# Linear attention, two blocks on one core: the second block's z finished at q's second unit, its sums behind G's last addition, its kv products two steps later

## The chip, the core and the metric

One NeuronCore of a Trainium2 chip runs the kernel. The metric is the device time of one execution in microseconds (us), given as the median of three timed executions. One further execution was taken with the hardware profiler; its rows are what this document reads. PE is the matrix engine (TensorE), DVE VectorE, ACT ScalarE, POOL GpSimd, SP SyncE. The last two issue most of the DMAs here; "SPq" rows are DMAs issued from SP's queue.

## The reference

Two independent blocks (A and B) of linear attention stand side by side; each has S = 2048 rows, D = 640 columns and H = 32 heads of 20 columns. Cut to what matters:

```
q, k, v = heads(x @ wqkv)
phi(t)  = where(t > 0, t + 1, exp(t)) + 1e-6
kv  = sum over s of phi(k)^T v          # per head, 20 x 20
z   = sum over s of phi(k)              # per head, 20
o   = (phi(q) @ kv) / (phi(q) . z + 1e-6)
out = o @ wo
result = concat(A, B)
```

## The kernel before

All large products run in a split form: each float32 operand is cut into a high and a low part of a reduced format, and three products (high x high, high x low, low x high) are added up in PSUM. So most PE work comes in threes.

**The first part** handles k of both blocks. For each pair of row tiles it forms phi(k) (tiles `ek`, then the split `pkh`, `pkl`), and gathers G = x^T phi(k) block by block: `gstep` (line 517) makes a product of 12 matmuls into a bank `psg`, and DVE adds the bank to `gacc` (line 537). The column sums of phi(k), from which z comes, are gathered by POOL DMAs that add `ek` to `zacc` in SBUF (line 406).

`zsums(b)` (line 592) turns `zacc` into z. Its steps: two DVE additions of halves (`zsum`, line 596); a DVE transpose (`zturn`, line 601); a DVE reduction (`zp`, line 602); a POOL DMA that writes `zp` to DRAM (`zd`, line 606); four POOL DMAs that read it back in another layout (`zq`, line 608); and `finish` (line 613), four small DVE instructions on lines 614 to 617 that make `z` and `zs`. Work of this first part is not emitted in the order written: `note` records jobs with their engine, cost and the tiles that they read and write, and `Plan.emit` lays them out by estimated due times. Its costs and due times set each engine's order, so an added dependence can move other jobs of the same engine.

**The second part** is written out by hand. `qmm(u, c)` (line 1069) computes one of five column blocks c of q for one of eight units u of 512 rows, in five steps k of three matmuls each (`psq`, lines 921 to 923). Units 0 to 3 belong to block A, 4 to 7 to block B. Behind each step, `run("q", u, c, k)` calls whatever `at(...)` placed there; so "(0,1,3)" below is the place behind unit 0, column block 1, step 3. Engines execute their instructions in program order, so an instruction that waits holds up all that stands behind it on the same engine.

Into unit 0 the kernel places block B's kv products: `kvmm2` (line 974) multiplies G by the weights of v for one of six groups of heads (`pskv`, line 981, shown in the trace as ten passes for five matmuls), in one of two PSUM banks (banks 5 and 6, tag "e"); DVE then takes the block diagonal (`kvt`, line 985), ACT and DVE split it (`kvh` line 915, `kvl` line 912). `mmm2` later multiplies the result by wo (`psm`), using a bank of tag "e" too. `wv`, the weights that `kvmm2` reads, stand in seven slots that the loads of unit 1's x (`xqs`, line 952) take over.

For each column block, ACT computes exp and relu of `psq` (lines 1089, 1090), DVE joins them to `pq` (line 1091), and `qacc` adds `pq` times z to `acc` (ACT line 1099 for c = 0, DVE line 1101 for the others). At the next unit's beginning `split_acc` splits `acc` into `ac` (ACT line 915, DVE line 912), and `denmm` makes the denominator from it on PE (`psd`, lines 1111 and 1112) at place (1,1,1). Units 0 to 3 read block A's z; block B's z is read for the first time in unit 4.

Of the kernel before, what the change touches and what calls it, by code (L numbers as in the profile page):

```python
# [12 lines left out]
OP = mybir.AluOpType  # L13
# [64 lines left out]
class Plan:  # L78
# [9 lines left out]
    def note(self, engine, n, fn, w, r, ahead=None, dma=None, late=None, by=None, due=None, safe=0.0, lat=0.0):  # L88
        base = self.RATE.get(engine)
        j = Job(engine, base[0] + base[1] * n if base else n, fn, ahead, dma)  # L90
        for part, writes in [(p, True) for p in w] + [(p, False) for p in r]:
            sp = part.space
            if sp.where is not None and sp not in j.spaces:
                j.spaces.append(sp)
            for lo, hi, other, wrote in sp.uses:
                if lo < part.hi and part.lo < hi and (writes or wrote) and other is not j:
                    j.deps.add(other)
            if writes:
                sp.uses = [u for u in sp.uses if not (part.lo <= u[0] and u[1] <= part.hi and u[2] is not j)]
            sp.uses.append((part.lo, part.hi, j, writes))  # L100
        for d in j.deps:
            d.nexts.append(j)
        for sp in j.spaces:
            sp.left += 1
        if engine == "PE":
            j.ideal = self.pe_at
            self.pe_at += j.cost
        j.late = self.pe_at + (25.0 if late is None else late)
        if by is not None:
            j.late = self.pe_at + by  # L110
        j.by, j.set, j.safe, j.lat = by, due, safe, (LAT if due is None else 1.9) + lat
        self.jobs.append(j)
        return j
# [105 lines left out]
def tile_linear_attn_pair(ctx: ExitStack, tc: tile.TileContext, ins, out: bass.AP):  # L219
# [3 lines left out]
    NC = D // P  # L223
    NT = S // P
    NG = NT // 4
    HF = D // 2
# [55 lines left out]
    note = plan.note  # L282
    MM, MMS = 0.147, 0.105

    G = {(b, c): Space(f"G{c}", D) for b in range(NB) for c in range(NC)}
# [3 lines left out]
    KZ = {b: Space("kz", 1) for b in range(NB)}  # L289
# [108 lines left out]
    zac = {}  # L398
# [118 lines left out]
    def gstep(i, h, c):  # L517
        b, g = divmod(i, NG)
        k = (3, 4, 5)[gn[0] % 3]
        gn[0] += 1  # L520
        tm, rd = [], []
        for j in range(4):
            n = 4 * i + j
            x = tuple(s[c * P:c * P + P] for s in xns[n])
            tm.append((x, pks[n][h]))
            rd += [*x, *pks[n][h]]
        note("PE", MM * 12, lambda: mms(tm, BK[k].open("psg")[:, :HF], True), [BK[k].all], rd)
        go = G[b, c][h * HF:h * HF + HF]

        def keep():  # L530
            if g == 0 and h == 0:
                gacc[b, c] = base.tile([P, D], F32, name="gacc", tag="gacc", bufs=NC)
            o = gacc[b, c][:, h * HF:(h + 1) * HF]
            if g == 0:
                act(o, BK[k].tile[:, :HF], AF.Copy)
            else:
                tt(o, BK[k].tile[:, :HF], o, op=OP.add)  # L537

        note("DVE" if g else "ACT", HF, keep, [go], [BK[k].all])
# [52 lines left out]
    def zsums(b):  # L592

        z, zt32 = Space("zsum", D, ANY), Space("zturn", D, ANY)
        for h in range(2):
            note("DVE", HF, lambda h=h: tt(z.all.f[:, h * HF:h * HF + HF], zac[b][h].all.f[:, :HF],
                                           zac[b][h].all.f[:, HF:], op=OP.add), [z[h * HF:h * HF + HF]], [zac[b][h].all], safe=6.0)
        part, four = Space("zpart", 20), Space("zfour", 20)
        pt, ft4 = zp[b]
        add = dict(axis=mybir.AxisListType.X, op=OP.add)  # L600
        note("DVE", D, lambda: nc.vector.transpose(zt32.all.f, z.all.f), [zt32.all], [z.all])
        note("DVE", D, lambda: nc.vector.tensor_reduce(
            pt.rearrange("p (g c) -> p c g", g=4), zt32.all.f.rearrange("p (c g t) -> p c g t", g=4, t=32), **add),
            [part.all], [zt32.all])
        zdv = Space("zd", 1)
        note("POOL", 1.0, lambda: nc.gpsimd.dma_start(zd[b], pt), [zdv.all], [part.all], dma=0.1, lat=2.0)
        for g in range(4):
            note("POOL", 1.0, lambda g=g: nc.gpsimd.dma_start(
                ft4[g * 32:g * 32 + 32].rearrange("p (q c) -> p q c", q=4),
                zd[b].rearrange("(q i) (g c) -> g i q c", q=4, g=4)[g]), [four[g:g + 1]], [zdv.all], dma=0.1, safe=6.0)  # L610
        zt, s = zz[b]

        def finish():
            nc.vector.tensor_reduce(zt, ft4.rearrange("p (q c) -> p c q", q=4), **add)
            nc.vector.tensor_scalar(zt, zt, S * EPS, None, op0=OP.add)
            nc.vector.tensor_reduce(s, zt, **add)
            nc.vector.tensor_scalar(s, s, EPS, EPS / 4, op0=OP.mult, op1=OP.add)

        note("DVE", 300, finish, [KZ[b].all], [four.all], safe=6.0)

    fd = {}

# [51 lines left out]
    a, z, x = jh[0][0:P], jl[0][0:P], jr[0][0:P]  # L674
# [117 lines left out]
    for p in range(4, NPB):  # L792
        i, h = divmod(p - 2, 2)
# [9 lines left out]
    for p in range(NPB + 1, NP):  # L803
        if p == NPB + 1:
            fl = kvs
        else:
            i, h = divmod(p - NPB - 2, 2)
            gready(NG + i)
            fl = filled(NG + i, h, *((LAST,) if p in (NPB + 2, NP - 1) else ()))
        for q, n, g, k in place:  # L810
            if q == p - NPB:
                fl.setdefault(n, []).append((mmm, g, k))
        kpair(p, fl)
        if p == NPB + 4:
            zsums(0)
        if p == NPB + 4:
            m_forms()
# [13 lines left out]
    for h in range(2):  # L831
        for c in range(NC):
            gstep(LG, h, c)
    zsums(1)

    wst, whl, wvt, xt, xts = {}, {}, {}, {}, {}

# [60 lines left out]
    def bank(name, tag="one", bufs=3):  # L898
        at, n = ptags[tag]
        pn[tag] = pn.get(tag, -1) + 1  # L900
        return psum.tile([P, 512], F32, name=name, tag=f"bank{at + pn[tag] % n}", bufs=1)
# [25 lines left out]
    def at(slot, f, *a):  # L927
        todo.setdefault(slot, []).append((f, a))
# [337 lines left out]

    for g in range(NGR):
        at(("q", 0, 0, 0), load_o, 1, g)
        at(("q", 0, (0, 0, 1, 1, 2, 2)[g], (0, 3, 0, 3, 0, 3)[g]), kvmm2, 1, g)
        at(("q", 0, 1 + g, 1) if g < 4 else ("q", 1, 0, 2 * g - 7), split_o, 1, g)  # L1270
        at((("q", 0, 2, 2), ("q", 0, 3, 2), ("q", 0, 4, 4), ("q", 0, 4, 4), ("q", 1, 1, 2), ("q", 1, 2, 2))[g], mmm2, 1, g)
        at((("q", 0, 2, 4), ("q", 0, 3, 4), ("q", 1, 0, 1), ("q", 1, 0, 3), ("q", 1, 1, 4), ("q", 1, 2, 4))[g],
           store_m, nc.gpsimd)
# [13 lines left out]
    h = NG - 1  # L1287
# [8 lines left out]
    for c in range(NC):  # L1296
        at(("q", 0, (0, 0, 1, 1, 2)[c], (1, 4, 1, 4, 1)[c]), load_xraw, 1, c)
        at(("q", 0, 4, c - 1) if c else ("q", 0, 3, 3), load_xq, 1, c)
        at(("q", 0, 4, c) if c else ("q", 0, 3, 4), round_xq, 1, c)
        for u in range(1, NU - 1):  # L1300
            at(("q", u, 3, c), load_xraw, u + 1, c)
            at(("q", u, 4, c), load_xq, u + 1, c)
            at(("o", u - 1, 2 * c + 4), round_xq, u + 1, c)

    den[0] = bank("psd", "small", 1)

# [93 lines left out]
```

## Time and profile before

| what | value |
|---|---|
| median of 3 timed executions | 579.86 us (579.19 to 580.07) |
| the profiled execution | 581.08 us |
| its span, first to last instruction | 579.3 us |
| busy PE / DVE / ACT / POOL | 567.1 / 434.3 / 341.4 / 63.1 us |
| DMA | 117.64 MB, mean 203 GB/s |
| mean granted PE clock | 0.994 |

The span is what the rows of the trace cover; what lies around it (581.08 - 579.3 = 1.78 us) is start and end of the program. A row of the timeline gives start, duration, engine, line, operation, the tiles, and in brackets the idle time of the engine before it with what ended it. Matmuls overlap in the pipeline, so the time that one takes out of PE is read from start to start rather than from its duration.

### The profile page before, as it was taken

How to read it: one execution, taken by the hardware profiler on the slowest of the kernel's cores; microseconds unless marked ns; L12 is line 12 of the kernel's file. 1: busy time of each engine (PE TensorE's matmuls, PEld its weight loads, DVE VectorE, ACT ScalarE, POOL GpSimd, SP SyncE). 2: the span in 40 equal slices, each digit the busy share in tenths (PEclk: the TensorE clock that was granted, in tenths of full speed). 3: DMA queues.
4: the chain of work that ended last, by engine and by line, in shares of the span. 5: the costliest groups of instructions: out<-in, count | busy, mean ns of one | idle time of the engine just before them, and what ended most of it. 6: DMA issues, size and time to landing. Idle time of an engine off the chain costs nothing.

```text
span 579.3 us, 9490 instructions
## 1 busy us (share of the span) xinstructions
PE 567.1 (98%) x3524; PEld 537.5 (93%) x3524; DVE 434.3 (75%) x706; ACT 341.4 (59%) x619; POOL 63.1 (11%) x103
## 2 busy tenths in 40 slices
PE   8999999999999999999959999999999999999997
PEld 6999999999999999999948889898998989898997
DVE  6788687698788758987615599967789776757792
ACT  6878566574787857676215765755657364545541
POOL 0210011110011111111010101211011200001010
PEclk9999999999999999999989999999999999999999
DMA  8994755858759488798956895664273996122022
GB/s 295 348 287 117 198 143 144 231 142 250 251 132 272 141 234 251 217 283 261 335 145 212 298 324 175 221 234 150 75 267 110 333 392 241 69 74 92 0 92 91
DMA packets 68321, 117.64 MB, mean 203 GB/s; under 512 B 6804, under 2 KB 30132, under 8 KB 68276
## 3 DMA queue, kind: packets, MB, share of 16 engines
q1 hardware_dynamic: 59060, 89.94, 47.5%
q0 software_dynamic: 8928, 26.92, 16.7%
q8 instruction: 27, 0.44, 0.3%
q10 hardware_dynamic: 288, 0.20, 0.1%
q14 instruction: 18, 0.15, 0.1%
HBM read 71.13 MB, written 35.41 MB: 184 GB/s over the span
## 4 chain that ended last, share of the span: by engine, by line
PE 95%; DMA 3%; DVE 1%; POOL 0%; SPq 0%; issue 0%; ACT 0%; DVEq 0%
PE psg L316 24%; PE pa L1200 12%; PE ka L316 10%; PE psq L921 8%; PE psq L922 8%; PE psq L923 8%; PE pe L1200 6%; PE ke L316 5%; PE psk L716 4%; PE psb L1200 4%; PE kb L316 3%; DMA zd<-zp 1%; DMA wk<-in_A_wk 1%; PE pskv L556 1%; PE psm L583 1%; PE pskv L981 1%
## 5 line engine op out<-in xcount | busy, mean ns | idle before, releaser
L316 PE MATMUL psg<-pkl,xnh 128*128 128x320 f32 x320 | 98.9, 309 | 0.0
L316 PE MATMUL psg<-pkh,xnh 128*128 128x320 f32 x320 | 98.8, 309 | 0.0
L316 PE MATMUL psg<-pkh,xnl 128*128 128x320 f32 x320 | 98.5, 308 | 0.0
L921 PE MATMUL psq<-xqh,wh 128*128 128x512 f32 x200 | 79.0, 395 | 0.0
L922 PE MATMUL psq<-xql,wh 128*128 128x512 f32 x200 | 78.4, 392 | 0.0
L923 PE MATMUL psq<-xqh,wl 128*128 128x512 f32 x200 | 78.3, 391 | 0.0
L316 PEld LDWEIGHTS psg<-pkl,xnh 128*128 128x128 f32 x320 | 60.1, 188 | 0.0
L316 PEld LDWEIGHTS psg<-pkh,xnl 128*128 128x128 f32 x320 | 60.1, 188 | 0.0
L316 PEld LDWEIGHTS psg<-pkh,xnh 128*128 128x128 f32 x320 | 60.0, 188 | 0.0
L489 ACT ACTIVATE kt<-ka 128x320 f32<-128x320 f32 x52 | 22.7, 437 | 54.4 <-PE ka L316 54.3
L1215 ACT ACTIVATE o<-pa 128x320 f32<-128x320 f32 x64 | 27.9, 438 | 45.3 <-PE pa L1200 45.0
L406 POOL DMA_DIRECT2D zacc<-ek x32 | 26.6, 842 | 236.6 <-DVE ek L499 173.6
L1091 DVE SCALAR_TENSOR_TENSOR pq<-eq,rq 128x512 f32<-128x512 f32 x40 | 27.6, 691 | 30.5 <-ACT rq L1090 30.4
L537 DVE TENSOR_TENSOR gacc<-psg,gacc 128x320 f32<-128x320 f32 x60 | 29.2, 489 | 23.9 <-PE psg L316 23.1
L1089 ACT ACTIVATE eq<-psq 128x512 f32<-128x512 f32 x40 | 23.9, 597 | 36.4 <-PE psq L923 34.1
L923 PEld LDWEIGHTS psq<-xqh,wl 128*128 128x128 f32 x200 | 37.8, 189 | 8.1
L921 PEld LDWEIGHTS psq<-xqh,wh 128*128 128x128 f32 x200 | 37.9, 190 | 7.3
L922 PEld LDWEIGHTS psq<-xql,wh 128*128 128x128 f32 x200 | 37.9, 189 | 7.2
L401 ACT ACTIVATE pkh<-ek,epst 128x640 fp32r<-128x640 f32 x32 | 26.5, 828 | 8.2 <-DVE ek L499 7.1
L1200 PE MATMUL pa<-fh,dah 128*128 128x320 f32 x96 | 29.7, 309 | 0.0
L1200 PE MATMUL pa<-fh,dal 128*128 128x320 f32 x96 | 29.7, 309 | 0.0
L1200 PE MATMUL pa<-fl,dah 128*128 128x320 f32 x96 | 29.7, 309 | 0.0
(215 smaller groups left out, 1560.1 us busy)
## 6 DMA issues: line engine op xcount, KB each, us to landing
zacc<-ek POOLq DMA_DIRECT2D x32, 320.0 KB, 4.9
xql<-xd SPq DMA_DIRECT2D x40, 256.0 KB, 4.8
xd<-xl SPq DMA_DIRECT2D x29, 320.0 KB, 4.2
out<-o POOLq DMA_DIRECT2D x28, 320.0 KB, 3.6
xns<-in_A_x SPq DMA_DIRECT2D x16, 320.0 KB, 5.4
xts<-in_B_xt_tiles SPq DMA_DIRECT2D x16, 320.0 KB, 3.8
xns<-in_B_x SPq DMA_DIRECT2D x16, 320.0 KB, 5.4
xqs<-in_A_xt SPq DMA_DIRECT2D x20, 256.0 KB, 5.9
```

The costliest lines, as they stand in the source:

```text
L316: nc.tensor.matmul(o, a.r, w.r, start=start and k == i == 0, stop=k == n - 1 and i == 2, skip_group_check=True)
L401: note("ACT", n + 110, lambda: act(hi.r, p.f, AF.Identity, bias=epst), [hi], [p, K0.all], by=8.0)
L406: note("POOL", 1.0, lambda: nc.gpsimd.dma_start(z.f, p.f, **kw), [z], [p], dma=1.0 if first else 1.86)
L537: tt(o, BK[k].tile[:, :HF], o, op=OP.add)
L716: nc.tensor.matmul(o[h][:, :HF], x[a].r, w[c][h * HF:h * HF + HF].r, start=c == 0 and i == 0, stop=c == NC - 1 and i == 2, skip_group_chec ...
L921: nc.tensor.matmul(o, whi, xhi, start=first, stop=False)
L922: nc.tensor.matmul(o, whi, xlo, start=False, stop=False)
L923: nc.tensor.matmul(o, wlo, xhi, start=False, stop=last)
L1089: nc.scalar.activation(e, ps, AF.Exp)
L1091: nc.vector.scalar_tensor_tensor(pq[u][:, c, :], e, 1.0, r, op0=OP.min, op1=OP.add)
L1200: nc.tensor.matmul(ps, x, y, start=start and n == i == 0, stop=n == len(terms) - 1 and i == 2, skip_group_check=True)
L1215: copy = lambda x, y: nc.scalar.activation(x, y, AF.Copy)
```

## The change

For block B alone (b = 1), the two `zsum` additions get a dependence on the last column block of G, so they stand behind the last addition to `gacc`. `finish` is no longer a job of the plan for block B: `zsums` returns it, and it is called at place (1,0,0), behind the first step of q's second unit. The six kv products move from the places (0,0,0), (0,0,3), (0,1,0), (0,1,3), (0,2,0), (0,2,3) to (0,0,2), (0,1,0), (0,1,3), (0,2,0), (0,2,3), (0,3,0).

```
-                                           zac[b][h].all.f[:, HF:], op=OP.add), [z[h * HF:h * HF + HF]], [zac[b][h].all], safe=6.0)
+                                           zac[b][h].all.f[:, HF:], op=OP.add), [z[h * HF:h * HF + HF]],
+                 [zac[b][h].all] + ([G[1, NC - 1].all] if b else []), safe=6.0)
...
-        note("DVE", 300, finish, [KZ[b].all], [four.all], safe=6.0)
+        if b == 0:
+            note("DVE", 300, finish, [KZ[b].all], [four.all], safe=6.0)
+        return finish
...
-    zsums(1)
+    z_end = zsums(1)
...
-        at(("q", 0, (0, 0, 1, 1, 2, 2)[g], (0, 3, 0, 3, 0, 3)[g]), kvmm2, 1, g)
+        at(("q", 0, (0, 1, 1, 2, 2, 3)[g], (2, 0, 3, 0, 3, 0)[g]), kvmm2, 1, g)
...
+    at(("q", 1, 0, 0), z_end)
```

Lines of the changed kernel have higher numbers behind the edit: `zturn` is line 602 there, `z` lines 615 to 618, `kvl` and `ac` line 915, `kvt` line 988, `pq` line 1094, `acc` line 1104, `psq` lines 924 to 926, `pskv` line 984.

DVE, from the last weight split of block A's q (`wl`) to the first products of unit 0, before:

```order
L858 TENSOR_TENSOR wl<-wq,wh 128x640
L537 TENSOR_TENSOR gacc<-psg,gacc 128x320 x2
L596 TENSOR_TENSOR zsum<-zacc 128x320
L601 STREAM_TRANSPOSE zturn<-zsum 128x640
L602 TENSOR_REDUCE zp<-zturn 128x5x4
L537 TENSOR_TENSOR gacc<-psg,gacc 128x320
L614 TENSOR_REDUCE z<-zq 128x5
L615 TENSOR_SCALAR z<-z 128x5
L616 TENSOR_REDUCE zs<-z 128x1
L617 TENSOR_SCALAR zs<-zs 128x1
L985 TENSOR_TENSOR kvt<-pskv,mask_74 120x120
L912 TENSOR_TENSOR kvl<-kvt,kvh 120x120
```

The same stretch of DVE now:

```order
L861 TENSOR_TENSOR wl<-wq,wh 128x640 x2
L537 TENSOR_TENSOR gacc<-psg,gacc 128x320 x4
L596 TENSOR_TENSOR zsum<-zacc 128x320 x2
L602 STREAM_TRANSPOSE zturn<-zsum 128x640
L603 TENSOR_REDUCE zp<-zturn 128x5x4
L988 TENSOR_TENSOR kvt<-pskv,mask_74 120x120
L915 TENSOR_TENSOR kvl<-kvt,kvh 120x120
L1094 SCALAR_TENSOR_TENSOR pq<-eq,rq 128x512
L988 TENSOR_TENSOR kvt<-pskv,mask_74 120x120
```

The last addition to `gacc` now stands ahead of the z reductions, the four instructions on z have left the place ahead of `kvt`, and `kvt` follows `zp` directly. On POOL and SP the order of the DMAs is unchanged.

DVE at the beginning of q's unit 1, now (before, the same rows stood there without the four on `z` and `zs`):

```order
L1094 SCALAR_TENSOR_TENSOR pq<-eq,rq 128x512
L1104 SCALAR_TENSOR_TENSOR acc<-pq,z,acc 128x512
L615 TENSOR_REDUCE z<-zq 128x5
L616 TENSOR_SCALAR z<-z 128x5
L617 TENSOR_REDUCE zs<-z 128x1
L618 TENSOR_SCALAR zs<-zs 128x1
L915 TENSOR_TENSOR ac<-acc,ac 128x512
L915 TENSOR_TENSOR wol<-wo,woh 80x640 x2
```

The four instructions now stand between the last addition to unit 0's `acc` and the split of it that `psd` needs.

PE at the start of q's unit 0, before: the first kv product behind the first step.

```order
L923 MATMUL psq<-xqh,wl 128x512
L981 MATMUL pskv<-gacc,wv 120x120 x5
L921 MATMUL psq<-xqh,wh 128x512
L922 MATMUL psq<-xql,wh 128x512
L923 MATMUL psq<-xqh,wl 128x512
```

And now: behind the third step.

```order
L924 MATMUL psq<-xqh,wh 128x512
L925 MATMUL psq<-xql,wh 128x512
L926 MATMUL psq<-xqh,wl 128x512
L984 MATMUL pskv<-gacc,wv 120x120 x5
L924 MATMUL psq<-xqh,wh 128x512
```

PE's number of matmuls is the same; two steps of `psq` have moved ahead of the first kv product, and each later product stands two or three steps further on.

## The prediction

> **What bounds the kernel now.** The page comes first: the busy times, and the chain of work that ended last.
>
> ```profile
> span 579.3 us, 9490 instructions
> ...
> PE 95%; DMA 3%; DVE 1%; POOL 0%; SPq 0%; issue 0%; ACT 0%; DVEq 0%
> ```
>
> PE is the bound almost everywhere, so only what takes time out of PE's stream can move the end. The table of waits, for PE over the whole span, says where that happens:
>
> ```profile
> PE pskv L981 <- DVE kvt L985: 6.3, 1, 6.3
> ...
> PE pskv L981 <- DVE gacc L537: 0.7, 1, 0.7
> ```
>
> There is one long wait and one short one, both at kv products of block B. (The table's two other entries lie at the kernel's start, where the change touches nothing.) The chain of waits between 287 and 302 us shows what the long one is made of (start, length, what):
>
> ```profile
> 287.10 0.85 DVE zturn L601
> ...
> 287.98 0.83 DVE zp L602
> ...
> 289.10 7.25 DMA zd<-zp
> ...
> 296.64 1.67 POOL zq L608 x3
> 298.31 2.01 DMA zq<-zd
> ...
> 300.40 0.20 DVE z L614
> ...
> 301.18 0.20 DVE kvt L985
> ```
>
> z goes out to DRAM in 7.25 us, comes back, and only then does DVE reach `kvt`. Nothing of `kvt` needs z: it stands behind `z` in DVE's program. The DVE timeline confirms it:
>
> ```profile
> 286.18 0.49 DVE L537 TENSOR_TENSOR gacc<-psg,gacc 128x320 f32<-128x320 f32 x1 [1.27 <-PE psg L316]
> ...
> 288.71 0.48 DVE L537 TENSOR_TENSOR gacc<-psg,gacc 128x320 f32<-128x320 f32 x1
> 300.40 0.19 DVE L614 TENSOR_REDUCE z<-zq 128x5 f32<-128x20 f32 x1 [11.21 <-DMA zq<-zd]
> ```
>
> DVE sat 11.21 us in front of `z`. With `kvt` unread, both PSUM banks of `pskv` stayed full, and PE stopped at the third product. The short wait has the same root: the last addition to `gacc` started at 288.71, behind `zturn` and `zp`, though PE had its sum ready by about 287.95 (286.18 plus the 1.76 us, 0.49 and 1.27, that one such addition follows another by).
>
> **What each stall costs.** PE's timeline, read from start to start:
>
> ```profile
> 287.74 0.39 PE L921 MATMUL psq<-xqh,wh 128*128 128x512 f32 x1
> ...
> 288.20 0.40 PE L923 MATMUL psq<-xqh,wl 128*128 128x512 f32 x1
> 289.25 1.31 PE L981 MATMUL pskv<-gacc,wv 128*120 128x120 f32 x10 [0.65 <-DVE gacc L537]
> ...
> 292.23 0.40 PE L923 MATMUL psq<-xqh,wl 128*128 128x512 f32 x1
> 292.47 1.21 PE L981 MATMUL pskv<-gacc,wv 128*120 128x120 f32 x10
> 293.44 0.48 PE L921 MATMUL psq<-xqh,wh 128*128 128x512 f32 x1
> ...
> 294.68 0.40 PE L923 MATMUL psq<-xqh,wl 128*128 128x512 f32 x1
> 301.42 2.36 PE L981 MATMUL pskv<-gacc,wv 128*120 128x120 f32 x10 [6.34 <-DVE kvt L985]
> 303.44 0.77 PE L921 MATMUL psq<-xqh,wh 128*128 128x512 f32 x1
> ...
> 306.02 0.40 PE L921 MATMUL psq<-xqh,wh 128*128 128x512 f32 x1
> ...
> 307.69 0.48 PE L921 MATMUL psq<-xqh,wh 128*128 128x512 f32 x1
> ...
> 309.16 0.88 PE L981 MATMUL pskv<-gacc,wv 128*80 128x80 f32 x10
> ```
>
> The product at 292.47 is the undisturbed one: 0.24 us behind the `psq` before it, 0.97 us until the next `psq`. Against it:
>
> - first stall: 289.25 - 288.20 = 1.05 instead of 0.24, so **0.81 us**, and its group lasts 1.31 instead of 1.21, so **0.10 us**;
> - second stall: 301.42 - 294.68 = 6.74 instead of 0.24, so **6.50 us**;
> - behind it PE runs slowly: the group takes 303.44 - 301.42 = 2.02 instead of 0.97, so **1.05 us**; the next six `psq` take 306.02 - 303.44 = 2.58 instead of the 309.16 - 307.69 = 1.47 that six take later, so **1.11 us**.
>
> That slowness is the clock, as the table by stretches shows (the column behind POOL's count is the granted PE clock, then DMA share and GB/s):
>
> ```profile
> 295.00:300.00 5.00, 0.08 (x1) 0.00 (x0) 0.00 (x0) 0.00 (x0) 2.23 (x4) 0.90 0.42 126
> 300.00:305.00 5.00, 3.58 (x14) 3.29 (x15) 2.60 (x10) 2.10 (x5) 0.00 (x0) 0.50 0.02 7
> 305.00:310.00 5.00, 5.00 (x34) 4.32 (x33) 1.83 (x5) 2.50 (x6) 0.00 (x0) 0.92 0.70 211
> ```
>
> The clock is 0.50 in the stretch in which PE starts again, and nearly full in the one behind it. Both stalls together cost 0.81 + 0.10 + 6.50 + 1.05 + 1.11 = **9.57 us**.
>
> [...]
>
> **The change part by part.**
>
> *The last addition to `gacc` ahead of the z sums.* It can run from about 287.95 to 288.45. Behind it come two `zsum` (0.41 each in the chain's rhythm, 286.18 + 0.49 to 287.10), `zturn` 0.85 and `zp` 0.83: `zp` is ready near 291.0 instead of 288.8. *The first product behind nine `psq`* starts at 287.74 + 9 x 0.23 = 289.8, so it finds `gacc` ready with 1.3 us to spare, and ends near 291.0. DVE then goes to `kvt` at once. The first stall goes whole: -0.91.
>
> *`finish` out of the way of `kvt`.* The banks of `pskv` are emptied as they fill. The third product, now at step (0,1,3), starts near 296; its bank was read by 291.5. So the second stall goes, and with it the slow stretch: -8.66.
>
> What is late next? The narrowest place that I find is the fifth product. It needs the bank of the second to last user of tag "e", the fourth product, which DVE reads behind the `pq` and `acc` of column block 1:
>
> ```profile
> 308.24 0.40 PE L923 MATMUL psq<-xqh,wl 128*128 128x512 f32 x1
> ...
> 309.85 0.69 DVE L1091 SCALAR_TENSOR_TENSOR pq<-eq,rq 128x512 f32<-128x512 f32 x1 [0.95 <-ACT rq L1090]
> 310.57 0.75 DVE L1101 SCALAR_TENSOR_TENSOR acc<-pq,z,acc 128x512 f32<-128x512 f32 x1
> 311.24 0.23 DVE L985 TENSOR_TENSOR kvt<-pskv,mask 80x80 f32<-80x80 f32 x1
> ```
>
> Here the last `psq` of column block 1 ends at 308.64 and the `kvt` behind `acc` starts 2.6 us later. Counting steps at 0.685 us (three `psq`), products at 1.06 (0.24 + 0.97 + 0.31 less two normal distances of 0.23) and one `psm` group at 0.9, block 1 now ends near 298.0, that `kvt` near 300.9, and the fifth product starts near 302.5: an estimate of 1.6 us to spare. If DVE or ACT were later than that, PE would wait for the rest.
>
> *`finish` at (1,0,0).* Four DVE instructions, 301.18 - 300.40 = 0.78 us, stand between the last `acc` of unit 0 and `ac`:
>
> ```profile
> 328.16 0.69 DVE L912 TENSOR_TENSOR ac<-acc,ac 128x512 fp32r<-128x512 f32 x1 [0.70 <-ACT ac L915]
> ...
> 328.91 0.51 PE L1112 MATMUL psd<-ac,same 128*128 128x512 f32 x1
> ```
>
> DVE idles 0.70 us there for ACT's half of the split, which covers all but about 0.1. The second `psd` starts as `ac` finishes, so it has no reserve; I charge the 0.1 in full: **+0.1**. Without that cover it would be 0.8.
>
> The cover also asks that z has landed. DVE reaches it near 328.16 - 0.70 - 9.6 = 317.8. `zp` at 291.0, `zd` issued 0.3 later, and then? Landing times of the two blocks' transfers (least, median, most), `zd` first, then `zq`:
>
> ```profile
> DMA to landing us min/median/max: 3.6/5.4/7.3
> ...
> DMA to landing us min/median/max: 1.9/2.2/3.4
> ```
>
> With the most of each and 2 us of POOL's issuing, z lands at 291.3 + 7.3 + 2 + 3.4 = 304. Nothing waits, with 14 us in hand. POOL's next DMA, the store of the first `psm`, comes near 303.5 and is not needed soon.
>
> *The moved `wv` reads.* Each product frees the slot for one `xqs` load, and SP's queue stands behind that. A product that is two steps later delays them by about 1.4 us against PE. The loads of the next unit that matter, `xql`, wait for PE anyway:
>
> ```profile
> L956 SPq DMA_DIRECT2D xql<-xd x4: 320/320/320, 319.3 to 321.3; - x4
> ...
> DMA to landing us min/median/max: 3.7/4.1/4.5
> ...
> 326.79 0.39 PE L922 MATMUL psq<-xql,wh 128*128 128x512 f32 x1
> ```
>
> The last is issued at 321.3, lands by 325.8 and is read at 326.79: 1 us to spare, unchanged against PE so long as DMA is not more crowded. Charged at nothing, bounds 0 and about 2 us.
>
> *The kv products' new places* add no matmul and cost nothing by themselves.
>
> **The sum**: -0.91 - 8.66 + 0.1 = -9.5. Made against the profiled execution, 581.08 - 9.5 = 571.6; the timed median is 1.22 lower, 579.86, and the same difference gives **570.4 us**. What the profile cannot say is whether that 1.22 lay in the stall. If all of it did, the gain of a timed run is 8.3 and the time 571.6; if a timed run's stall holds a `zq` that takes 3.4 instead of 2.0, the gain is 1.4 larger, 569.0.
>
> **The rivals.**
>
> *Part comes back as new short waits at the products* (12%). For it: 288 to 304 us, where DVE and ACT idled, now hold all their work, and the margin at the fifth product is 1.6 us by estimate. Against it: the same sequence of `kvt`, `pq`, `acc` ran behind 303 us without a wait of PE. A lateness of 2.6 to 4 would leave 1 to 2.4 us: 571.4 to 572.8.
>
> *The next unit's x is late* (8%). DMA was nearly empty at 300 to 305 (share 0.02); that pause goes, and the `xql` have 1 us. With landings of 5.5 to 7.5 us instead of 4.5, PE waits 0 to 2 us: up to 572.4.
>
> *Nothing is gained, the time is given back later* (3%): were the later units paced by DMA, the end would stay, 579.9. Against it: the table of waits has no PE wait for a DMA behind 302.
>
> *Slower* (3%). DVE now meets z's transfer in front of `ac`, which PE's `psd` needs, and DVE is busy all through the transfer. If z landed behind 317.8, PE would wait as long, and if long enough, restart slowly as before (2.2 us). Landing 7.4 us late, at 325.2, it would eat the 9.6 gained; at 330 the time would be 584.8. Against it: landings sum to 304, and block A's `zd`, written while DVE was busy, took the 3.6 us, not the 7.3. [...]
>
> **How the numbers follow.** The forecast has 74%, with its own range 569.0 to 571.6; the first two rivals reach to 572.8. The range takes them in: 569.0 to 572.8. The chances go by what a measurement of this kernel can tell from no change, 0.2% or 1.2 us: faster holds the forecast and the two rivals that give part back, 94%; same 3%, slower 3%.
>
> **What would show it.** In the changed profile, right: no PE wait at `pskv`; PE clock full from 285 to 310; the last `gacc` addition near 288; `z` on DVE near 317 with no wait for a DMA ahead of it; unit 1's first `psq` near 314 instead of 323.8, and the rest of the trace shifted by the same 9.5. Wrong: a PE wait at the fifth product (first rival), at `xql` (second), at `psd` (slower), or a later wait for a DMA that takes the shift back.

## The result, and the profile after

| | time, median | range | executions |
|---|---|---|---|
| before | 579.53 us | 578.64 to 580.07 | 4 |
| changed kernel | 570.62 us | 570.45 to 571.33 | 4 |

The ratio is 0.985, with a 95% interval of 0.9833 to 0.9867. The forecast was 570.4, in a range of 569.0 to 572.8.

The page of the changed kernel's profiled execution (570.47 us), its span, PE's busy time, and the shares of the chain that ended last:

```profile
span 568.7 us, 9491 instructions
...
PE 564.2 (99%) x3524; PEld 536.0 (94%) x3524; DVE 434.3 (76%) x706; ACT 341.2 (60%) x619; POOL 62.9 (11%) x103
...
PE 99%; DVE 0%; issue 0%
```

The DMAs have left the chain. The table of waits for PE has one entry left in the whole kernel, at its start:

```profile
PE psi L647 <- DVE ones L324: 1.0, 1, 1.0
```

PE's timeline through unit 0, first `psq`, the six kv products, first `psq` of unit 1 (start, length, line, tiles, passes):

```profile
286.69 0.39 PE L924 MATMUL psq<-xqh,wh 128*128 128x512 f32 x1
...
288.77 1.21 PE L984 MATMUL pskv<-gacc,wv 128*120 128x120 f32 x10
...
291.91 1.21 PE L984 MATMUL pskv<-gacc,wv 128*120 128x120 f32 x10
...
295.04 1.21 PE L984 MATMUL pskv<-gacc,wv 128*120 128x120 f32 x10
...
297.48 1.21 PE L984 MATMUL pskv<-gacc,wv 128*120 128x120 f32 x10
...
301.51 0.88 PE L984 MATMUL pskv<-gacc,wv 128*80 128x80 f32 x10
...
303.63 0.88 PE L984 MATMUL pskv<-gacc,wv 128*80 128x80 f32 x10
...
313.20 0.40 PE L924 MATMUL psq<-xqh,wh 128*128 128x512 f32 x1
```

No row has an idle bracket, and each product of 120 columns has the undisturbed length of 1.21 us. Unit 0, from its first `psq` to unit 1's, lasts 313.20 - 286.69 = **26.51 us**. Before it lasted from 287.74 to 323.81, **36.07 us**; this is the first `psq` of unit 1 in the trace of before:

```profile
323.81 0.40 PE L921 MATMUL psq<-xqh,wh 128*128 128x512 f32 x1
```

The difference, 9.56 us, is the effect in unit 0. Nothing of it is given back: at unit 1's start the changed kernel is 10.61 us ahead, and its span is shorter by the same 10.6. The other 1.05 us were there before unit 0, which this execution reached earlier: near the kernel's start the PE of before waited 0.7 us for weights, which this one did not. Nothing shows that the change has a part in this: the eight kernels below, with and without its parts, reach unit 0 between 286.98 and 287.54.

The table by stretches, in the two stretches in which PE stood still or ran slowly before (granted clock, DMA share and GB/s at the end):

```profile
295.00:300.00 5.00, 5.00 (x34) 4.42 (x33) 2.96 (x6) 1.52 (x4) 2.22 (x4) 1.00 0.74 211
300.00:305.00 5.00, 5.00 (x39) 4.47 (x38) 2.25 (x5) 2.81 (x7) 0.64 (x1) 1.00 0.89 250
```

PE is busy throughout at clock 1.00, and DMA, which had a share of 0.02 from 300 to 305, now has 0.89. DVE's timeline, at the start of unit 0 and at the start of unit 1:

```profile
286.88 0.49 DVE L537 TENSOR_TENSOR gacc<-psg,gacc 128x320 f32<-128x320 f32 x1 [1.27 <-PE psg L316]
287.29 0.88 DVE L596 TENSOR_TENSOR zsum<-zacc 128x320 f32<-128x320 f32 x2
...
289.09 0.82 DVE L603 TENSOR_REDUCE zp<-zturn 128x20 f32<-128x640 f32 x1
290.02 0.28 DVE L988 TENSOR_TENSOR kvt<-pskv,mask 120x120 f32<-120x120 f32 x1
...
316.09 0.75 DVE L1104 SCALAR_TENSOR_TENSOR acc<-pq,z,acc 128x512 f32<-128x512 f32 x1
316.76 0.19 DVE L615 TENSOR_REDUCE z<-zq 128x5 f32<-128x20 f32 x1
...
317.38 0.15 DVE L618 TENSOR_SCALAR zs<-zs 128x1 f32<-128x1 f32 x1
317.55 0.69 DVE L915 TENSOR_TENSOR ac<-acc,ac 128x512 fp32r<-128x512 f32 x1
```

`kvt` follows `zp` as soon as the first product is there. The four instructions on z run at 316.76 without a wait for a DMA, and `ac` follows at once. POOL's timeline shows the transfers of z, and below it stands the landing time of the four `zq` (least, median, most):

```profile
290.21 0.58 POOL L607 DMA_DIRECT2D zd<-zp  x1 [20.27 <-DVE zp L603]
297.17 2.22 POOL L609 DMA_DIRECT2D zq<-zd  x4 [6.39 <-DMA zd<-zp]
...
DMA to landing us min/median/max: 3.2/3.8/5.8
```

The way out takes about as long as before (297.17 - 290.21 = 6.96 until POOL goes on, where it was 7.54); the way back is slower (it was 2.0). Loads that used to wait behind PE's stall now run beside it, as the DMA shares above show; that they are what slows it is likely, but no run tests it alone. z lands by 304.6 at the latest (the last `zq` is issued at 298.8, the longest takes 5.8), 12 us ahead of its use.

### The profile page after: what moved, and what is told of

The parts are those of the page before. It is cut to its first block, busy times and chain, and to the rows that moved or that the text cites. A ratio compares the mean times of both kernels' runs of the same rounds, so it can differ in the third digit from the quotient of the medians.

```text
span 568.7 us, 9491 instructions
## 1 busy us (share of the span) xinstructions
PE 564.2 (99%) x3524; PEld 536.0 (94%) x3524; DVE 434.3 (76%) x706; ACT 341.2 (60%) x619; POOL 62.9 (11%) x103
## 4 chain that ended last, share of the span: by engine, by line
PE 99%; DVE 0%; issue 0%
PE psg L316 25%; PE pa L1203 12%; PE ka L316 10%; PE psq L924 8%; PE psq L925 8%; PE psq L926 8%; PE pe L1203 6%; PE ke L316 5%; PE psk L719 4%; PE psb L1203 4%; PE kb L316 3%; PE pskv L556 1%; PE pskv L984 1%; PE psm L583 1%; PE psi L647 1%; PE psk L696 1%
```

## The experiments

The theory: PE stopped because DVE, which has to empty the `pskv` banks, stood at z's transfer; the change lets the transfer run beside PE. The rivals: the later places of the products give PE its room; or the late addition to G is the main cost; or the slow running behind the stall has another cause than the idle clock. All lengths of unit 0 below are read as above, in one profiled execution each.

**`finish` alone.** Only the call of `finish` is moved to (1,0,0); sums and products are as before.

```
-        note("DVE", 300, finish, [KZ[b].all], [four.all], safe=6.0)
+        if b == 0:
+            note("DVE", 300, finish, [KZ[b].all], [four.all], safe=6.0)
+        return finish
...
+    at(("q", 1, 0, 0), z_end)
```

> The kernel before with finish of block B moved to (1,0,0) alone; sums and products stay where they were. Theory (the long stall is DVE standing at z): the long stall and its slow clock go, 8.66 us, the short wait for the last addition to G stays, 0.91 us: unit 0 (first psq of unit 0 to first psq of unit 1, 36.07 us before and 26.51 us with the whole change) lasts 27.3 to 27.5 us, time 571.2 to 571.7 us. Rival (the later products are what gives PE room): most of the stall stays, unit 0 above 32 us, time above 576 us.

Measured: 572.14 us (571.92 to 572.44), ratio 0.9863 (0.9844 to 0.9881). Unit 0 lasts 314.96 - 287.54 = 27.42 us. Its PE timeline, first `psq` of unit 0, first and third product, first `psq` of unit 1:

```profile
287.54 0.39 PE L924 MATMUL psq<-xqh,wh 128*128 128x512 f32 x1
...
289.06 1.31 PE L984 MATMUL pskv<-gacc,wv 128*120 128x120 f32 x10 [0.66 <-DVE gacc L537]
...
294.73 1.21 PE L984 MATMUL pskv<-gacc,wv 128*120 128x120 f32 x10
...
314.96 0.40 PE L924 MATMUL psq<-xqh,wh 128*128 128x512 f32 x1
```

The long stall is gone, 36.07 - 27.42 = 8.65 us, with the products at their old places. The short wait is left, 27.42 - 26.51 = 0.91 us. The median is 0.4 us above what was expected; the unit's length is inside.

**The products alone.** Only the places change:

```
-        at(("q", 0, (0, 0, 1, 1, 2, 2)[g], (0, 3, 0, 3, 0, 3)[g]), kvmm2, 1, g)
+        at(("q", 0, (0, 1, 1, 2, 2, 3)[g], (2, 0, 3, 0, 3, 0)[g]), kvmm2, 1, g)
```

> The kernel before with the kv products moved to their later places alone. Theory: the short wait goes (0.91 us), the third product is reached later, at 8.35 us from unit 0's start instead of 7.18, and still waits until DVE is past z, so the wait falls from 6.5 to about 5.3 us and the slow clock stays: unit 0 about 34 us, time 577.3 to 578.0 us. Rival (the later products are what gives PE room): unit 0 below 30 us, time below 573.5 us.

Measured: 577.54 us (576.5 to 579.87), ratio 0.9958 (0.9944 to 0.9972). The profiled execution took 579.47 us, 1.9 above the median; in it unit 0 lasts 34.89 us. PE's timeline at the third product, and the stretches behind it:

```profile
301.13 2.36 PE L981 MATMUL pskv<-gacc,wv 128*120 128x120 f32 x10 [5.27 <-DVE kvt L985]
```

```profile
300.00:305.00 5.00, 3.87 (x14) 3.49 (x15) 2.50 (x10) 2.91 (x6) 0.00 (x0) 0.54 0.05 18
305.00:310.00 5.00, 5.00 (x26) 4.51 (x25) 3.19 (x8) 2.39 (x6) 0.00 (x0) 0.78 0.73 207
```

The wait is the 5.3 us expected, and the median lies where it was expected. The unit is 0.9 us longer than expected because PE ran slowly for longer: 0.78 from 305 to 310, where the kernel before had 0.92. The later places alone are worth 1.2 us by the units of the two profiled executions and 2.9 us by the medians (580.39 - 577.54). The timed runs say where much of this difference lies: seven of the twelve had a mean granted clock of 0.997 (576.5 to 578.1 us), the other five, the profiled one among them, 0.993 or 0.994 (577.55 to 579.87 us), which is also what nearly all runs of the kernel before had. Against those, the five with their median of 578.54 us are 1.9 us faster.

**The sums alone.** The `zsum` additions go behind G's last addition; `finish` stays in front of `kvt`.

```
-                                           zac[b][h].all.f[:, HF:], op=OP.add), [z[h * HF:h * HF + HF]], [zac[b][h].all], safe=6.0)
+                                           zac[b][h].all.f[:, HF:], op=OP.add), [z[h * HF:h * HF + HF]],
+                 [zac[b][h].all] + ([G[1, NC - 1].all] if b else []), safe=6.0)
```

> The kernel before with the sums of z behind G's last addition alone; finish still stands ahead of kvt. Theory: z starts 2.2 us later, so DVE passes z 1.5 to 2.2 us later (the transfer to DRAM may be a little faster), the short wait falls to 0.1 us, the long one grows: unit 0 37.5 to 38.3 us, time 581.0 to 581.8 us, slower than before. Rival (the addition to G standing behind the sums is the main cost): unit 0 shorter than before, time below 579 us.

Measured: 581.5 us (580.22 to 583.05) beside 580.39 of the kernel before, ratio 1.0021 (1.0008 to 1.0033); unit 0 lasts 37.48 us. The table of waits for PE:

```profile
PE pskv L981 <- DVE kvt L985: 7.8, 1, 7.8
```

This edit by itself makes the kernel slower: it starts the transfer later, and the transfer is what PE waits for.

**The whole change with one part taken back**, first the products, then the sums (the reverse of the two diffs above).

> The changed kernel with the kv products back at their old places. Theory: the first product is reached 0.69 us from unit 0's start, about when the last addition to G ends, so PE waits 0.1 to 0.2 us there and nowhere else: unit 0 26.6 to 26.8 us, time 570.7 to 571.0 us, the same as the whole change. Rival (the later products are needed for the gain): unit 0 above 27.4 us, time above 571.5 us.

Measured: 570.93 us (570.61 to 571.62), ratio 0.9843 (0.9824 to 0.9861); unit 0 lasts 26.66 us. PE's timeline there: the first product starts 0.28 us behind the `psq` before it at 287.45, instead of 0.24, and lasts 1.31 instead of 1.21.

```profile
287.73 1.31 PE L984 MATMUL pskv<-gacc,wv 128*120 128x120 f32 x10
```

> The changed kernel with the sums of z back ahead of G's last addition. Theory: that addition then ends near 1.5 us from unit 0's start, the first product is reached at 2.06 us, so nothing waits: unit 0 26.5 us, time 570.5 to 570.8 us, the same as the whole change; of the two edits that remove the short wait either is enough. Rival (the later sums are needed): a wait of PE at the first product of 0.3 us or more.

Measured: 570.9 us (570.27 to 571.23), ratio 0.9834 (0.9816 to 0.9853); unit 0 lasts 26.52 us. DVE's last addition to `gacc`, then PE's first product:

```profile
288.44 0.48 DVE L537 TENSOR_TENSOR gacc<-psg,gacc 128x320 f32<-128x320 f32 x1
```

```profile
289.55 1.21 PE L984 MATMUL pskv<-gacc,wv 128*120 128x120 f32 x10
```

Either part alone takes the short wait away once `finish` is out of the way; the second one adds 0.15 us or nothing.

**A filler in the stall.** The kernel before, with 28 matmuls of no use ahead of the third product; their result is read by nobody.

```
         w = wvt.pop((b, g))
+        if g == 2:
+            fill = bank("psf", "a", 2)
+            fw, (fx, _) = whl["q", 0, 0][0], xt[0, 0]
+            for i in range(28):
+                nc.tensor.matmul(fill, fw[:, :P], fx, start=True, stop=True)
```

> The kernel before with 28 matmuls of no use (128x512 each, into a bank nobody reads) ahead of the third kv product, in the time in which PE stood idle; nothing else is changed and z keeps its place. Theory (the 2.16 us of slow running behind the stall are the clock, lowered by the idle time): the clock stays at 1.00 from 295 to 310 us, unit 0 is 2.0 to 2.4 us shorter, 33.7 to 34.1 us, time 577.2 to 577.7 us. Rival (the slow running comes from the crowd on DVE, ACT or the memory behind the stall): unit 0 stays at 36.1 us, time 579.5 us.

Measured: 579.15 us (578.47 to 579.72) beside 579.89 of the kernel before, ratio 0.9982 (0.9973 to 0.9992): the median misses the expectation, 577.2 to 577.7, by 1.5 us, and every run lies above it; unit 0 lasts 34.45 us, 1.62 less than before, where 2.0 to 2.4 was expected. Its PE timeline, the stretches, and the table of waits:

```profile
294.17 6.53 PE L982 MATMUL psf<-xqh,wh 128*128 128x512 f32 x28
301.09 1.31 PE L986 MATMUL pskv<-gacc,wv 128*120 128x120 f32 x10 [0.39 <-DVE kvt L990]
```

```profile
295.00:300.00 5.00, 5.00 (x24) 4.14 (x23) 0.00 (x0) 0.00 (x0) 2.23 (x4) 1.00 0.26 65
300.00:305.00 5.00, 4.61 (x30) 3.75 (x29) 2.60 (x10) 2.43 (x6) 0.00 (x0) 1.00 0.17 42
```

```profile
PE psq L922 <- DMA xql<-xd: 1.0, 1, 1.0
```

The clock stays at 1.00 through the same wait, and the product behind it is no longer slow: 1.31 instead of 2.36. So the slow running was the clock. Two things took from the gain: z came 0.4 us later than in the other execution (the third product starts 14.11 us after the unit's start instead of 13.68), and in unit 1 PE met the last `xql` before it had landed and waited 1.0 us. That is the second rival of the prediction. The load was not started later against PE: it was issued at 319.0, 5.4 us ahead of the moment (324.40) at which PE would have read it, and that distance was 5.5 us in the kernel before (321.3 to 326.79) and in the changed one (310.7 to 316.18). But PE could read it only at 325.60, 6.6 us behind its issue. Why it took longer here is not shown: the landings of `xql` that this trace has took 4.0 to 4.2 us.

**`finish` early.** The changed kernel with the call moved back to (0,1,4).

```
-    at(("q", 1, 0, 0), z_end)
+    at(("q", 0, 1, 4), z_end)
```

> The changed kernel with finish at (0,1,4), behind the third product and ahead of pq of column block 1, some 15 us earlier on DVE. Theory (what counts is whether z has landed when DVE comes to it): DVE comes to it near 297.3 us and waits until z lands, 301 to 304 us, so the kvt that the fifth product needs is 2 to 5 us late: PE waits there 2 to 4.5 us, with up to 2 us of slow clock on top if the wait is long, unit 0 28.5 to 33 us, time 572.5 to 577 us. Rival (finish costs only its own 0.8 us wherever it stands): unit 0 below 27.3 us, time below 571.5 us.

Measured: 576.84 us (574.24 to 579.01), ratio 0.995 (0.9931 to 0.9968): the median lies at the upper end of the expected 572.5 to 577. The profiled execution, 578.91 us, is 2.1 above it; in it unit 0 lasts 34.30 us, above the 28.5 to 33 expected. Its DVE and PE timelines:

```profile
305.13 0.19 DVE L615 TENSOR_REDUCE z<-zq 128x5 f32<-128x20 f32 x1 [7.22 <-DMA zq<-zd]
```

```profile
307.54 1.62 PE L984 MATMUL pskv<-gacc,wv 128*80 128x80 f32 x10 [5.18 <-DVE kvt L988]
```

The mechanism is the expected one, and the fifth product is where it shows; in this execution z landed about 1 us later than the upper bound that the expectation had, and the slow clock came on top. The fastest of the ten runs, 574.24 us, had a mean granted clock of 1.000, so it had next to no slow clock, with the same order of instructions. Most of the gain hangs on how far behind the transfer `finish` stands.

**z late.** The changed kernel, with z sent out and back three more times before it is used; the values are the same.

```
+        for i in range(BOUNCE if b else 0):
+            note("POOL", 1.0, lambda: nc.gpsimd.dma_start(pt, zd[b]), [part.all], [zdv.all], dma=0.1, lat=2.0)
+            note("POOL", 1.0, lambda: nc.gpsimd.dma_start(zd[b], pt), [zdv.all], [part.all], dma=0.1, lat=2.0)
```

(BOUNCE is 3.)

> The changed kernel with six more small DMAs in z's way (out and back three times), so that z lands some 20 to 30 us later, behind the point at which DVE comes to it. Theory (the change has moved the wait to where it has 14 us of slack, not removed it): DVE stands at z in front of ac, PE stands at the second psd for as long as z lands behind 316.8 us, and restarts with about 2.2 us of slow clock: time 570.6 plus that wait plus 2.2, for a landing at 320 to 330 us 574 to 586 us. Rival (z is far from the path anywhere in block A's units): time 570.6 us.

Measured: 586.58 us (586.3 to 587.24), ratio 1.011 (1.0094 to 1.0126). Its DVE and PE timelines, and one stretch:

```profile
330.23 0.19 DVE L619 TENSOR_REDUCE z<-zq 128x5 f32<-128x20 f32 x1 [12.63 <-DMA zq<-zd]
```

```profile
331.65 0.80 PE L1119 MATMUL psd<-ac,same 128*128 128x512 f32 x1 [12.53 <-DVE ac L919]
```

```profile
330.00:335.00 5.00, 3.35 (x10) 2.80 (x11) 4.67 (x9) 1.25 (x2) 0.00 (x0) 0.50 0.58 220
```

The wait has come back at the second `psd`, 12.5 us long, with a slow restart, and the kernel is slower than before. The sum that the expectation gave, 570.6 + 12.5 + 2.2 = 585.3, is 1.3 us short; z landed just behind the 330 that it allowed for, and the slow clock lasted longer than in the kernel before (below). So the change has given the transfer cover; it has not made z cheaper.

**The slow restart in all of these.** For each kernel with a stall, the unit's length less that of the same order without one (in brackets), less the delay of the product that waited, counted from the unit's start, is what the slow clock cost:

| kernel (without the stall) | longer by | delay | slow clock |
|---|---|---|---|
| before (`finish` alone) | 36.07 - 27.42 = 8.65 | 13.68 - 7.19 = 6.49 | 2.16 |
| products alone (sums back) | 34.89 - 26.52 = 8.37 | 13.79 - 8.36 = 5.43 | 2.94 |
| sums alone (products back) | 37.48 - 26.66 = 10.82 | 14.40 - 6.43 = 7.97 | 2.85 |
| `finish` early (whole change) | 34.30 - 26.51 = 7.79 | 20.18 - 14.82 = 5.36 | 2.43 |
| filler (`finish` alone) | 34.45 - 27.42 = 7.03 | 14.11 - 7.19 = 6.92 | 0.11 |

Why the last column differs is in the traces. The granted clock reads 0.50 already when PE restarts, and it stays there for a time that differs; in the kernel before it reads 0.50 from 299.0, 2.4 us ahead of the restart. The kernel before, then the products alone, from the restart to the end of the low clock:

```profile
301.42:305.84 4.42, 4.42 (x16) 3.94 (x17) 2.02 (x6) 2.93 (x7) 0.00 (x0) 0.50 0.16 39
301.13:307.23 6.10, 6.09 (x23) 5.50 (x24) 2.81 (x8) 4.17 (x9) 0.00 (x0) 0.50 0.30 79
```

For the sums alone it is 5.96 us, for `finish` early 5.11, for z late 6.36. At that clock one `psq` follows another by 0.42 to 0.43 us (304.02 to 304.87 in the kernel before), instead of 0.23, so PE loses about half of such a stretch, an estimate: 2.21, 3.05, 2.98 and 2.56 us for the four stalled rows of the table, each within 0.13 of its last column.

Each row is one execution, and the loss is not the same in every run of a kernel. A mean granted clock that is 0.003 higher, as in seven runs of the products alone, means about 3.5 us less at the clock of 0.50 (0.003 x 578 / 0.50, an estimate). The rows for the products alone and for `finish` early come from executions above the median of their kernel (579.47 against 577.54, 578.91 against 576.84).

## Why the prediction was right, point by point

- *The long stall, 8.66 us*: `finish` alone gave 8.65. That it was DVE standing at z, and not the places of the products, is shown by that run and by the products alone, which kept a wait of 5.3 us.
- *The slow clock within it, 2.16 us*: shown by the filler, which kept PE's clock at 1.00 through the wait and left 0.11. The four stalled kernels of the table lost 2.16 to 2.94. The mean clocks of the timed runs show that other runs lost less.
- *The short wait, 0.91 us*: 27.42 - 26.51 = 0.91. The prediction gave the gain to the addition that moved ahead and noted the margin that the later product adds; the runs show that either is enough, and that the sums moved without `finish` cost about 1 us (ratio 1.0021).
- *The 0.1 us charged at `psd`*: a term that was mis-sized, it measures nothing. In the changed kernel the second `psd` starts 0.29 us behind the first (318.00 and 318.29), before it was 0.30. DVE's four instructions end at 317.38 + 0.15 = 317.53, just when ACT's half of the split ends (316.88 + 0.63 = 317.51), so the cover is whole, but has nothing to spare.
- *The fifth product with 1.6 us to spare*: the `kvt` that it needs ends at 299.56 + 0.28 = 299.84, the product starts at 301.51, 1.67 later. `finish` early used this margin up, and PE waited exactly there.
- *z landed with 14 us in hand*: it was 12. The way back took up to 5.8 us, where the prediction took 3.4 for its most: a size that it had wrong, without a consequence here. In the profile of `finish` early, where it had one, the way back took up to 5.7 us.
- *The next unit's x unchanged*: no wait in the changed kernel, and the last `xql` is issued as far ahead of its read as before, 5.5 us. The margin of 1 us is not shown. The prediction took 4.5 us for the last landing, but that is the longest that the trace has, and the trace has no landing for the last `xql`. The filler, with the same distance, lost 1.0 us there, so the margin can be used up.
- *The slower rival*: its place (`psd` behind `ac` behind z) and price were right when z was made late on purpose; with a z as it is, the landing is 12 us from it.
- *The open question whether the 1.22 us between the profiled execution and the median lay in the stall*: it stays open, since only one execution of before was profiled. Medians of before were 579.53, 580.39 and 579.89 in the three series, so the gain is 8.9 to 9.8 us against 570.62, around the 9.56 of the unit's length. The mechanism and its terms held; that the time itself came out within 0.2 us of the forecast is in part luck, since runs of before lie anywhere from 578.6 to 581.8 us. Those of the changed kernel lie within 0.9 us.

Left open: what sets, in a given run, how much of the low clock falls behind the restart; why the `zq` take longer beside other loads; and why the last `xql` came late in the filler.

## What to carry to other kernels

When PE waits for an engine that empties its banks, look at what that engine stands at, and whether the waiting work needs it at all: here one small instruction, waiting for a round trip through DRAM whose result is first read more than 100 us later (by ACT in unit 4, at 421.33 in the changed kernel's trace), cost 1.5% of the kernel. Move the use behind the work that covers the round trip, count the slack to the next place that waits for that engine, and price a PE stall of several microseconds at its length plus the slow clock behind it, 2.16 to 2.94 us behind the stalls of 5.2 to 7.8 us in the table. Undo the parts one at a time: of three edits here one carried nearly all, the other two were each other's spare, and one was harmful by itself.

## What the runs showed that was not expected

- The slow clock behind a stall cost 2.16 to 2.94 us in the table, not a fixed amount, after idle stretches of 5.2 to 7.8 us; the highest cost came behind a stall of 5.3 us, and the filler, with no such idle stretch, left 0.11. The low clock as a whole lasted 6.8 us in the kernel before (299.0 to 305.8) and 13.6 us for z late (324.4 to 338.0); it began 3.9 and 5.3 us after PE's last row ahead of the stall had ended (295.08 and 319.13). What sets where it begins and ends is not shown.
- The same small `zq` DMAs landed in 1.9 to 2.0 us in the kernel before and for the sums alone, in which PE stood still while they were under way; in 2.0 to 3.5 us in the filler; in 3.2 to 5.8 us in the changed kernel; and in 4.0 to 5.7 us for `finish` early. Removing the stall went with a slower way back of the transfer that had caused it.
- Saving PE time can be partly given back at the next wait: the filler's 1.6 us in unit 0 became 0.6 us behind `xql`, which came 1.0 us late. The changed kernel saves far more and does not pay this.
